# Sliding-window attention with a gated MLP: postponing the low parts of weights while VectorE has a result bank to empty, and a scratch buffer for each head's maxima

## The chip, the cores and the metric

The kernel runs on one core of a Trainium2 chip. A core has a matrix engine (TensorE, PE in the profile; its weight loads are shown as PEld), VectorE (DVE), ScalarE (ACT), GpSimd (POOL) and SyncE (SP), which here issues nearly all DMAs. Each engine works through its own queue in order; engines wait for each other, and for DMAs, through semaphores. The metric is the device time of one execution in microseconds, lower is better.

## The reference

```python
def _A_ref(x, wqkv, wo):                      # S = 2048, D = 640, H = 32, Dh = 20, W = 256
    qkv = (x @ wqkv).reshape(B, S, 3, H, Dh).transpose(2, 0, 3, 1, 4)
    scores = einsum("bhqd,bhkd->bhqk", q, k) * (Dh ** -0.5)
    mask = (idx[:, None] - idx[None, :] >= 0) & (idx[:, None] - idx[None, :] < W)
    p = softmax(where(mask, scores, -1e9))
    o = einsum("bhqk,bhkd->bhqd", p, v)
    return o.transpose(0, 2, 1, 3).reshape(B, S, D) @ wo

def _B_ref(x, w1, b1, w2, b2):                # F = 1536
    h = relu(x @ w1 + b1) ** 2
    return h @ w2 + b2

xn = layernorm(x)
return x + _A_ref(xn, wqkv, wo) * silu(_B_ref(xn, w1, b1, w2, b2))
```

All data are float32.

## The kernel before

Products are made from split numbers: every operand has a high part, rounded by ScalarE (a copy into fp32r), and a **low part**, the rest, made by VectorE or GpSimd (`raw - high`). A product takes three matmuls: high by high, high by low, low by high.

A first stage (to about 113 us) normalizes and transposes x, makes v and the first q and k. Then comes one long stage in which two kinds of work are interleaved on TensorE. The attention goes through 16 pairs of heads with 16 query tiles each, one tile a step of about 2 us: `scores` (L650) makes the scores of both heads of the pair in two banks `sps`; `maxima` (L658) on VectorE adds the mask and takes the row maximum, into the tile `mt`; its elementwise output `junk` is read by nobody. In the profile each maximum is two VectorE instructions: the pass itself and a read of the accumulator. Thirteen steps later `scores_t` makes transposed scores (`stps`, L690), `exps` on ScalarE (L696) and masks on GpSimd (L697, L699) make the probabilities, and every eight or so steps `values` (L731) does a burst of matmuls into the bank `ops`. A score bank is used again in the next step, so TensorE waits there for the maximum of the step before.

Between these, `filler` does the dense products in pieces: q and k of the later heads (`qkps`), the first layer of the MLP (`hps`) and the second (`yps`), all at L640 as halves of 64 rows, in three banks that take turns. A `Job` holds the second halves of a group; when its last one has been given out, `done` puts the bank's evacuation 0.25 (`SOON`) later. For `yps` the evacuation is `ysb = yps + bias` (or plus the first half's result, `yin`), on VectorE (L1185); for `qkps` it is `shm` on ScalarE (L1077) and `slo` on VectorE (L1080); for `hps` ScalarE (L1150). A group can start only when its bank has been emptied. After the loop a last stage makes the output product with wo (`wops`, from about 759 us).

The order on all engines is written out when the program is built, by a clock in the kernel's own code that adds up estimated costs (`clock`). `later(wait, fn)` puts a function down for a time of that clock, and `soon()` runs what is due. Weights arrive as pieces: `start_pieces` issues the load into one of three `raw` buffers (SyncE, L976), `go` makes the high part on ScalarE (L988, L997), and `subtract` puts the low parts (L991, L998) down for 1.9, 2.6, 3.3 ... after that, in `lows`. A raw buffer is free when all low parts of its piece have been made. `state[2]` is the step, 10**6 after the loop.

Of the kernel before, what the change touches and what calls it, by code (L numbers as in the profile page):

```python
# [11 lines left out]
BF16 = mybir.dt.bfloat16  # L12
# [3 lines left out]
P = 128  # L16
# [40 lines left out]
SOON = 0.25  # L57
# [9 lines left out]
def attn_mlp_kernel(ctx: ExitStack, tc, x, wqkv, wo, w1, b1, w2, b2, out):  # L67
# [9 lines left out]
    def mm_bank(shape, name):  # L77
        turn[0] = (turn[0] + 1) % 3
        return pmm.tile(shape, F32, tag=f"mm{turn[0]}", name=name)
# [62 lines left out]
    with tc.tile_pool(name="ph1v", bufs=2) as p1v, tc.tile_pool(name="ph1", bufs=2) as p1, tc.tile_pool(name="ph1x", bufs=4) as p1b, tc.tile_pool(name="ph1w", bufs=1) as p1w, tc.tile_pool(name="ph1t", bufs=2, space=PSUM) as p1t:  # L142
# [286 lines left out]
        with tc.manual_schedule(engines={E_.PE, E_.Activation, E_.DVE, E_.Pool, E_.SP}):  # L429
# [90 lines left out]
            for w in "kq":  # L520
                ps = pat.tile([P, BT // 2], F32, tag="s", name="qkps")
# [7 lines left out]
            for b in range(NB):  # L529
# [27 lines left out]
                for w in "kq":  # L557
                    ps = mm_bank([P, BT], "qkps")
# [25 lines left out]
    at2 = ctx.enter_context(tc.tile_pool(name="at2", bufs=2))  # L584
# [10 lines left out]
    backlog = deque()  # L595
    class Job:

        def __init__(self, done):
            self.items, self.after, self.done = deque(), None, done

    def put(j, emit, cost):
        clock[2] = clock[j]
# [21 lines left out]
    def drain(queue, jobs=99):  # L624
        end = max(0, len(queue) - jobs)
        while len(queue) > end:
            assert queue[0].after is not None
            behind(queue)
# [24 lines left out]

    def maxima(p, q, ss, nk):
        for hh in range(2):
            junk = at2.tile([P, 3 * P], BF16, tag="junk", bufs=1, name="junk")
            m = MG * hh + q % MG
            nc.vector.tensor_tensor_reduce(out=junk[:, :nk], in0=ss[hh][:, :nk], in1=mask[:, 3 * P - nk:], scale=1.0, scalar=-3.0e38, op0=ALU.add, op1=ALU.max, accum_out=mts[q // MG % 2][:, m:m + 1])  # L658

# [86 lines left out]
    state = [0.0, 0.0, 0]  # L746
# [3 lines left out]
    def post(dst, src, wait=0.0, then=lambda: None):  # L750
        def go():
            posts.append((dst, src))
            then()
        if whole[0] or not wait:
            go()
        else:
            later(wait, go)

    def post_all():
        for dst, src in posts:  # L760
            nc.sync.dma_start(dst, src)
        posts.clear()
# [9 lines left out]
    def later(wait, fn):  # L772
        tasks.append((clock[0] + wait, len(tasks), fn))
# [14 lines left out]
    def next_task():  # L788
        clock[0] = max(clock[0], min(tasks)[0])
        soon()  # L790
# [14 lines left out]
    def room():  # L805
        while state[2] < 10 ** 6 and not (banks and banks[0][0] < clock[0] + PATIENCE):
            yield None
# [17 lines left out]
    def halves(job, ps, a, b_, first, last, o=0, n=None):  # L825
        n = n or ps.n
        cost, out = COST[n], ps.tile[:, o:o + n]

        def front():
            job.mark = half(0, out, a, b_, start=first, stop=False)  # L830

        def back():
            if first:
                wait_for(job.mark)
            half(1, out, a, b_, start=False, stop=last)
        ahead(front, cost)
        job.items.append((back, cost))
        if last:
            job.after = clock[0]

    def open_job(evac, *then):
        def done():
            later(SOON, lambda: (post_all(), evac()))
            for f in then:
                f()
        job = Job(done)
        backlog.append(job)
        return job

    def mm_halves(ps, mms, work, evac, *then):  # L850
        job = open_job(evac, *then)
        for j, (a, b_) in enumerate(mms):
            halves(job, ps, a, b_, j == 0, j == len(mms) - 1)
            yield work
# [9 lines left out]
    def lin1(tiles, off, n):  # L864
        t, o = divmod(off, KC * BT)
        return tiles[t][:, o:o + n]
# [80 lines left out]
            item[1]()  # L947

    lows = []

    def subtract(tag, jobs):
        left = [len(jobs)]

        def put_off(k, job):
            def go():
                if item in lows:
                    lows.remove(item)
                    job()
                    left[0] -= 1
                    if not left[0]:  # L960
                        held[0] -= 1
            item = (tag, go)
            lows.append(item)
            later(1.9 + 0.7 * k, go)
        for k, job in enumerate(jobs):
            put_off(k, job)

# [83 lines left out]
    def filler():  # L1051
# [6 lines left out]
        for g, b in order_qk:  # L1058
# [9 lines left out]
            for w in "qk":  # L1068
                hi, lo = (t() for t in ws[g][w])
                yield from room()  # L1070
                ps = Acc(BT, "qkps")
# [13 lines left out]
                then = []  # L1085
                if b == 0 and w == "q":
                    then = [lambda g=g: shut.discard(f"g{g + 1}")]
                elif w == "k":
                    then = [lambda t=t: shut.discard(t) for t in opens.get((g, b), ())]
# [7 lines left out]
        def load_yin(i):  # L1097
            if i < NT:
                t = order[i]
                assert (0, t) in stored_y  # L1100
                yins[t] = wgt.tile([P, D], F32, tag="wgkh", name="yin")
                nc.sync.dma_start(yins[t], y_d[0][:, t, :])
        xb, its = [xT[p][NB - 1] for p in range(2)], []

        def late():
            j = lates[0]
            lates[0] += 1
            if j >= 3:
                load(0)
            if j >= 5:  # L1110
                load(1)
            if j >= 7:
                load(2)

        for n, (hf, b) in enumerate(blocks):
# [22 lines left out]
            for m, u in enumerate(parts):  # L1138
                yield from room()
                ps = Acc(BT, "hps")  # L1140
# [19 lines left out]
                job = open_job(evac, *([used] if m == len(parts) - 1 else []))  # L1160
# [10 lines left out]
            for tt in range(4):  # L1171
                t = b * 4 + tt
                place = [None]
                jobs = []

                def start(nh, hf=hf, t=t, place=place, idx=4 * (n - NB) + tt, end=n == NB - 1 and tt == 3, n=n, tt=tt):
                    sl = slice(nh * HALF, (nh + 1) * HALF)
                    ps = Acc(HALF, "yps")

                    def evac():  # L1180
                        vload[0] += 0.5
                        if not nh:
                            place[0] = room_of("p32", "ysb") if n == last else wgt.tile([P, D], F32, tag="wgqh", name="ysb")
                        ysb = place[0]
                        nc.vector.tensor_add(ysb[:, sl], ps.tile, (yins[t] if hf else b2t)[:, sl])  # L1185
                        ps.free(1.2)
                        if nh:
                            if n == last:
                                ybt[t] = ysb
                            else:  # L1190
                                post(y_d[hf][:, t, :], ysb, 1.0, lambda: stored_y.add((hf, t)))
                            if hf:
                                del yins[t]
                                load_yin(idx + 2)
                            if end:
                                shut.discard("21")
                    return [ps, open_job(evac), 0]

                def product(jb, nh, fc):
                    ps, job, _ = jb  # L1200
                    u = fc if fc < WIDE else (tt // 2, fc // 2)
                    o = tt * P if fc < WIDE else fc % 2 * MT + tt % 2 * P
                    while u not in made:
                        if state[2] < 10 ** 6:
                            yield None
                        elif tasks:
                            next_task()
                        else:
                            drain(backlog, 1)
                    for hp, wp in ((0, 0), (0, 1), (1, 0)):  # L1210
                        jb[2] += 1
                        halves(job, ps, hs[u][hp][:, o:o + P], lin1(wt2, (wp * NFH + fc) * D + nh * HALF, HALF), jb[2] == 1, jb[2] == 3 * NFH)
                        yield 0.133
                for nh in range(2):
                    yield from room()
                    if n == last:
                        late()
                    job = start(nh)
                    for fc in (*range(WIDE, NFH), *range(WIDE)) if tt < 2 else range(NFH):
                        yield from product(job, nh, fc)  # L1220
# [40 lines left out]
    def room_of(tag, name):  # L1261
        if tag == "p32":
            return at2.tile([P, 2, 3 * P], F32, tag="p32", bufs=PBUF, name=name).rearrange("p a n -> p (a n)")[:, :D]
        return wgt.tile([P, D], F32, tag=tag, name=name)
# [135 lines left out]
    due = [0.0]  # L1400
# [15 lines left out]
    with tc.manual_schedule(engines={E_.PE, E_.Activation, E_.DVE, E_.Pool, E_.SP}):  # L1416
# [7 lines left out]
        for s in range(steps):  # L1424
# [29 lines left out]
            if a:  # L1454
                maxima(*a, *sc)
# [51 lines left out]
```

## Time and profile before

| | us |
|---|---|
| median of 3 runs | 837.44 (837.16 to 837.87) |
| profiled execution | 838.13 |
| its span, first to last instruction | 836.4 |
| TensorE's granted clock | 1.0 throughout |

The profile is of the one execution of 838.13 us; its moments are microseconds from the start of its span. Lines such as L658 are lines of the kernel before; names are the kernel's own. "out<-in" tells what an instruction writes and reads. In a row of the order of time stand the start, the duration, the engine, the line and the operation, and in brackets how long the engine had been idle before it and who ended that; rows of equal neighbours are merged and carry their count. "2 us <- DVE" is an inference from semaphore events: where an instruction waits for several, it is put down to the latest event.

### The profile page before, as it was taken

Reading aid. Unit: us, or ns where it says so; the run is one execution under the profiler, and the core shown is the slowest. Engines: PE = TensorE matmul, PEld = TensorE weight load, DVE = VectorE, ACT = ScalarE, POOL = GpSimd, SP = SyncE. Lnnn points to the kernel's source line nnn. Section 1 sums busy time; section 2 is a strip of 40 time slices with the busy share of each in tenths; the row PEclk is TensorE's granted clock in tenths of the full one; section 3 lists DMA queues with packets and bytes.
Section 4 is the critical chain, followed back from the end, with each engine's and each line's share of the span. In section 5 each row is a group of like instructions: output and inputs, shape, how many; then the busy total and the mean of one; then the engine's idle time right before and its main releaser. Section 6 shows DMA issues by size and latency. Waiting matters only on the chain.

```text
span 836.4 us, 25137 instructions
## 1 busy us (share of the span) xinstructions
PE 826.2 (99%) x10082; PEld 779.0 (93%) x10082; DVE 477.8 (57%) x1398; ACT 425.5 (51%) x760; POOL 364.2 (44%) x672
## 2 busy tenths in 40 slices
PE   8999999999999999999999999999999999999997
PEld 8999999989889999999999989999999999999997
DVE  7855457656578455455455476655455455246763
ACT  6254323545566744744754754844644744664321
POOL 5177900334344542533542543643543643552442
PEclk9999999999999999999999999999999999999999
DMA  6999577878697555546083536585266557346962
GB/s 236 299 390 348 182 215 269 238 260 282 232 324 262 142 173 156 127 157 174 21 268 130 121 108 181 134 244 176 59 222 172 130 177 224 92 131 199 373 251 80
DMA packets 88812, 166.40 MB, mean 199 GB/s; under 512 B 10232, under 2 KB 36472, under 8 KB 87672
## 3 DMA queue, kind: packets, MB, share of 16 engines
q1 hardware_dynamic: 88536, 164.63, 62.7%
q8 instruction: 79, 1.29, 0.7%
q14 instruction: 37, 0.30, 0.1%
q10 hardware_dynamic: 160, 0.16, 0.1%
HBM read 93.66 MB, written 70.52 MB: 196 GB/s over the span
## 4 chain that ended last, share of the span: by engine, by line
PE 94%; DVE 2%; DMA 2%; issue 1%; ACT 1%; SPq 0%; POOL 0%; DVEq 0%; POOLq 0%; ACTq 0%
PE hps L640 20%; PE yps L640 20%; PE qkps L640 13%; PE ops L731 10%; PE wops L800 8%; PE stps L690 5%; PE sps L650 4%; PE vps L239 4%; PE qkps L214 3%; PE vps L362 3%; PE tps L181 1%; DVE junk L658 1%; DMA k_d<-slo 1%; DMA qs<-q_d 1%; PE vps L417 0%
## 5 line engine op out<-in xcount | busy, mean ns | idle before, releaser
L658 DVE CUSTOM_DVE_ANT_0 junk<-sps,mask 128x384 bf16<-128x384 f32 (+2 forms) x512 | 272.4, 532 | 250.9 <-PE sps L650 91.3
L696 ACT ACTIVATE p<-stps 128x768 f32<-128x768 f32 (+2 forms) x256 | 197.5, 772 | 255.5 <-PE stps L690 236.6
L697 POOL TENSOR_SCALAR_AFFINE_SELECT p<-p 128x256 f32<-128x256 f32 x256 | 109.8, 429 | 336.4 <-ACT p L696 334.0
L640 PE MATMUL yps<-w,hh 64*128 64x320 f32 x1536 | 226.1, 309 | 2.2 <-DVE ysb L1185 2.0
L640 PE MATMUL hps<-xb,w 64*128 64x256 f32 (+1 forms) x2100 | 210.0, 304 | 0.0
L640 PEld LDWEIGHTS hps<-xb,w 64*128 64x128 f32 x2100 | 194.7, 186 | 3.5 <-issue 2.7
L640 PEld LDWEIGHTS yps<-w,hh 64*128 64x128 f32 x1536 | 187.9, 185 | 7.3 <-DVE ysb L1185 4.4
L640 PE MATMUL yps<-w,hl 64*128 64x320 f32 x768 | 179.3, 308 | 0.0
L650 PE MATMUL sps<-ks,qs 60*128 60x384 f32 (+2 forms) x512 | 125.4, 335 | 1.0 <-DVE mt L658 1.0
L690 PE MATMUL stps<-qs,ks 62*128 62x384 f32 (+2 forms) x512 | 122.0, 334 | 0.1
L640 PEld LDWEIGHTS yps<-w,hl 64*128 64x128 f32 x768 | 121.4, 185 | 0.4 <-issue 0.4
L640 PE MATMUL qkps<-xT,wgqh 64*128 64x512 f32 x320 | 99.4, 391 | 0.0
L640 PE MATMUL qkps<-xT,wgkh 64*128 64x512 f32 x320 | 98.2, 391 | 0.0
L699 POOL TENSOR_SCALAR_AFFINE_SELECT p<-p 128x256 f32<-128x256 f32 x224 | 95.5, 426 | 0.0
L731 PE MATMUL ops<-p,vp 128*21 128x128 f32 (+1 forms) x2128 | 86.6, 311 | 0.0
L731 PEld LDWEIGHTS ops<-p,vp 128*21 128x21 f32 x2128 | 63.6, 101 | 21.2 <-issue 6.3
L650 PEld LDWEIGHTS sps<-ks,qs 60*128 60x128 f32 x512 | 78.4, 185 | 4.3 <-DVE mt L658 2.2
L690 PEld LDWEIGHTS stps<-qs,ks 62*128 62x128 f32 x512 | 77.5, 187 | 0.7 <-ACT p L696 0.6
L1155 POOL TENSOR_TENSOR hl<-sq,hh 128x512 fp32r<-128x512 f32 x48 | 62.1, 1293 | 16.1 <-ACT sq L1154 15.5
L800 PE MATMUL wops<-wo,oT 128*128 128x320 f32 (+2 forms) x384 | 62.0, 310 | 0.0
L640 PE MATMUL qkps<-xT,wgkl 64*128 64x512 f32 x160 | 61.4, 393 | 0.0
L640 PE MATMUL qkps<-xT,wgql 64*128 64x512 f32 x160 | 61.4, 390 | 0.0
(163 smaller groups left out, 1234.2 us busy)
## 6 DMA issues: line engine op xcount, KB each, us to landing
ks<-k_d SPq DMA_DIRECT2D x64, 240.0 KB
qs<-q_d SPq DMA_DIRECT2D x64, 240.0 KB
xb<-xs SPq DMA_DIRECT2D x60, 256.0 KB
k_d<-shm SPq DMA_DIRECT2D x20, 512.0 KB
q_d<-shm SPq DMA_DIRECT2D x20, 512.0 KB
xs<-xT SPq DMA_DIRECT2D x8, 1280.0 KB
y<-ysb SPq DMA_DIRECT2D x28, 320.0 KB
o<-osb SPq DMA_DIRECT2D x64, 128.0 KB
```

The costliest lines, as they stand in the source:

```text
L214: nc.tensor.matmul(ps, wt[:, c, :], xT[part][b][:, c * BT + t0:c * BT + t0 + n], start=m == 1, stop=m == 3 * KC)
L239: nc.tensor.matmul(ps, xT[xp][b][:, c * BT + t * P: c * BT + (t + 1) * P], wv[wp][:, c, nh * HALF:(nh + 1) * HALF], start=first and m == 0 ...
L640: return nc.tensor.matmul(out, a[r], b_[r], skip_group_check=True, **kw)
L650: nc.tensor.matmul(ss[hh][:, :nk], qs[i][o, q * P:(q + 1) * P], ks[i][o, k0 * P:k0 * P + nk], start=True, stop=True)
L658: nc.vector.tensor_tensor_reduce(out=junk[:, :nk], in0=ss[hh][:, :nk], in1=mask[:, 3 * P - nk:], scale=1.0, scalar=-3.0e38, op0=ALU.add, o ...
L690: nc.tensor.matmul(tps[:, hh, :n], ks[i][o, kb * P:(kb + 1) * P], qs[i][o, kb * P:kb * P + n], start=True, stop=True)
L696: nc.scalar.activation(p32[:, :, :n], tps[:, :, :n], AF.Exp, scale=SCALE)
L697: nc.gpsimd.affine_select(p32[:, :, 0:P], p32[:, :, 0:P], pattern=[[0, 2], [1, P]], compare_op=ALU.is_ge, fill=0.0, base=0, channel_multip ...
L699: nc.gpsimd.affine_select(p32[:, :, 2 * P:], p32[:, :, 2 * P:], pattern=[[0, 2], [-1, P]], compare_op=ALU.is_gt, fill=0.0, base=0, channel ...
L731: nc.tensor.matmul(ot[r0:r0 + VW, c0:c0 + len(part), :], vps[p][:, kb // 4, kb % 4, hh, :], pts[p, kb][:, hh, :].rearrange("p (t n) -> p t ...
L800: nc.tensor.matmul(ps, a, b_, start=j == 0, stop=j == n - 1)
L1155: nc.gpsimd.tensor_sub(hh[1][:, :BT], sq, f32(hh[0]))
```

## The change

`maxima` gives each of the two heads a scratch buffer of its own, `junk0` and `junk1`, in place of one `junk`. Jobs of `yps` are marked `vector`. While such a job's evacuation is due but not yet given out (`vector_evacs`), or while the oldest waiting job is one of them with less than 0.7 of second halves left, `pressing()` is true, and a low part that comes due is put down again for 0.4 later. `ensure`, which forces low parts out ahead of their use, calls `go()` without `due` and isn't put off. After the loop nothing is put off.

```diff
-            junk = at2.tile([P, 3 * P], BF16, tag="junk", bufs=1, name="junk")
+            junk = at2.tile([P, 3 * P], BF16, tag=f"junk{hh}", bufs=1, name="junk")
...
-    def open_job(evac, *then):
+    def open_job(evac, *then, vector=False):
+        def finished():
+            post_all()
+            evac()
+            vector_evacs[0] -= vector
+
         def done():
-            later(SOON, lambda: (post_all(), evac()))
+            vector_evacs[0] += vector
+            later(SOON, finished)
             for f in then:
                 f()
         job = Job(done)
+        job.vector = vector
...
+    vector_evacs = [0]
+
+    def pressing():
+        job = backlog[0] if backlog else None
+        return state[2] < 10 ** 6 and (vector_evacs[0] or job and job.vector and job.after is not None and sum(c for _, c in job.items) < 0.7)
 
     def subtract(tag, jobs):
         left = [len(jobs)]
 
         def put_off(k, job):
-            def go():
+            def go(due=False):
                 if item in lows:
+                    if due and pressing():
+                        later(0.4, lambda: go(True))
+                        return
                     lows.remove(item)
...
-            later(1.9 + 0.7 * k, go)
+            later(1.9 + 0.7 * k, lambda: go(True))
...
-                    return [ps, open_job(evac), 0]
+                    return [ps, open_job(evac, vector=True), 0]
```

On TensorE, ScalarE, GpSimd and SyncE every instruction stands where it stood. Only VectorE's queue differs. Of its 512 maxima, 512 named VectorE's own semaphore (DVE_49) among what they wait for, and now 23 do; with that, 488 of VectorE's instructions that only wait are gone. And low parts change places with `ysb` in three spots. In the rows, `ISA` with `junk` is a maximum, `ISA` with `mt` alone its accumulator read; `w_1_1` are tiles of MLP weights; line numbers of the changed kernel are 15 higher from L991 on.

VectorE near 485 us of the profile, before:

```order
L658 ISA junk,mt_101<-sps,mask 128x384 [waits DVE_49,PE_49]
L658 ISA mt_101 128x1
L658 ISA junk,mt_101<-sps,mask 128x384 [waits DVE_49,PE_49]
L658 ISA mt_101 128x1
L991 TENSOR_TENSOR w_1_1_8514<-raw,w_1_0_8470 128x384 [waits DMAHW6_49,Activation_49]
L991 TENSOR_TENSOR w_1_1_8514<-raw,w_1_0_8470 128x384
L1185 TENSOR_TENSOR ysb<-yps,b2t 128x320 [waits DMAHW5_49,PE_49]
```

and now:

```order
L658 ISA junk,mt_101<-sps,mask 128x384 [waits PE_49]
L658 ISA mt_101 128x1
L658 ISA junk,mt_101<-sps,mask 128x384 [waits PE_49]
L658 ISA mt_101 128x1
L1200 TENSOR_TENSOR ysb<-yps,b2t 128x320 [waits DMAHW5_49,PE_49]
L1006 TENSOR_TENSOR w_1_1_8530<-raw,w_1_0_8470 128x384 [waits DMAHW6_49,Activation_49]
L1006 TENSOR_TENSOR w_1_1_8530<-raw,w_1_0_8470 128x384
```

The two maxima no longer wait for VectorE itself, and the `ysb` went ahead of two low parts. Near 497 us a `ysb` went ahead of one low part in the same way. The third spot is VectorE near 735 us, before:

```order
L998 TENSOR_TENSOR wo_13552<-raw,wo_13551 128x640
L1185 TENSOR_TENSOR ysb<-yps,yin 128x320
L998 TENSOR_TENSOR wo_13552<-raw,wo_13551 128x640 x2
L1185 TENSOR_TENSOR ysb<-yps,yin 128x320
L1256 RECIPROCAL rec<-rec 128x128
```

and now:

```order
L1200 TENSOR_TENSOR ysb<-yps,yin 128x320
L1013 TENSOR_TENSOR wo_13552<-raw,wo_13551 128x640 x2
L1200 TENSOR_TENSOR ysb<-yps,yin 128x320
L1271 RECIPROCAL rec<-rec 128x128
L1013 TENSOR_TENSOR wo_13552<-raw,wo_13551 128x640
```

Three low parts of wo each went behind the `ysb` next to them, the third behind a reciprocal too. TensorE near 320 us, the same in both kernels:

```order
L640 MATMUL yps<-w_0_2_3948,hh 128x320
L650 MATMUL sps<-ks_1473,qs_1472 128x384 [waits DMAHW1_49,DMAHW0_49,DVE_49]
L650 MATMUL sps<-ks_1473,qs_1472 128x384 [waits DMAHW3_49,DMAHW2_49,DVE_49]
L690 MATMUL stps<-qs_116,ks_117 128x384 [waits Activation_49]
L690 MATMUL stps<-qs_116,ks_117 128x384
L665 MATMUL stps<-ident,mt_100 64x64 x2
```

Here the scores of a new half of a pair begin; their matmuls wait for the loads of q and k (DMAHW) beside VectorE. Nothing moved there.

More of the change, by code (lines that the diff above doesn't have):

```diff
@@ L598, in __init__ @@
         def __init__(self, done):
-            self.items, self.after, self.done = deque(), None, done
+            self.items, self.after, self.done, self.vector = deque(), None, done, False
     def put(j, emit, cost):
```

## The prediction

> **What bounds the kernel now.** I read the page first, for the busiest engine and the chain that ended last; then the list of waits; then the order of time around each wait of TensorE.
>
> ```profile
> span 836.4 us, 25137 instructions
> PE 826.2 (99%) x10082; PEld 779.0 (93%) x10082; DVE 477.8 (57%) x1398; ACT 425.5 (51%) x760; POOL 364.2 (44%) x672
> PE 94%; DVE 2%; DMA 2%; issue 1%; ACT 1%; SPq 0%; POOL 0%; DVEq 0%; POOLq 0%; ACTq 0%
> ```
>
> TensorE is busy for 826.2 of 836.4 us and the chain lies on it for 94%. Its work is the same after the change, and so is its order. VectorE works 57% of the span, so making it faster is worth nothing by itself: the change can give back only idle time of TensorE that VectorE ends. The list of waits names that time (total, times, longest):
>
> ```profile
> PEld yps L640 <- DVE ysb L1185: 4.4, 9, 1.3
> PEld sps L650 <- DVE mt L658: 2.2, 5, 1.0
> ```
>
> I count the idle time of PEld, the weight load, since a matmul that waits begins by loading its weights. The ceiling is thus 4.4 + 2.2 = 6.6 us, 0.8% of the time. Here are the 14 waits one by one, from the order of time; in the brackets stands how long the load waited, and for whom:
>
> ```profile
> 159.71 0.18 PEld L650 LDWEIGHTS sps<-ks,qs 60*128 60x128 f32 x1 [0.28 <-DVE mt L658]
> 245.63 0.18 PEld L650 LDWEIGHTS sps<-ks,qs 60*128 60x128 f32 x1 [0.53 <-DVE mt L658]
> 320.02 0.18 PEld L650 LDWEIGHTS sps<-ks,qs 60*128 60x128 f32 x1 [0.96 <-DVE mt L658]
> 364.49 0.29 PEld L640 LDWEIGHTS yps<-w,hh 64*128 64x128 f32 x3 [0.30 <-DVE ysb L1185]
> 377.67 0.18 PEld L640 LDWEIGHTS yps<-w,hh 64*128 64x128 f32 x1 [0.40 <-DVE ysb L1185]
> 428.88 0.19 PEld L640 LDWEIGHTS yps<-w,hh 64*128 64x128 f32 x2 [0.18 <-DVE ysb L1185]
> 438.92 0.18 PEld L640 LDWEIGHTS yps<-w,hh 64*128 64x128 f32 x1 [0.26 <-DVE ysb L1185]
> 488.00 0.18 PEld L640 LDWEIGHTS yps<-w,hh 64*128 64x128 f32 x1 [1.26 <-DVE ysb L1185]
> 495.33 0.18 PEld L640 LDWEIGHTS yps<-w,hh 64*128 64x128 f32 x1 [0.72 <-DVE ysb L1185]
> 505.24 0.18 PEld L640 LDWEIGHTS yps<-w,hh 64*128 64x128 f32 x1 [0.59 <-DVE ysb L1185]
> 560.39 0.29 PEld L640 LDWEIGHTS yps<-w,hh 64*128 64x128 f32 x3 [0.44 <-DVE ysb L1185]
> 617.97 0.19 PEld L640 LDWEIGHTS yps<-w,hh 64*128 64x128 f32 x2 [0.21 <-DVE ysb L1185]
> 647.38 0.18 PEld L650 LDWEIGHTS sps<-ks,qs 60*128 60x128 f32 x1 [0.20 <-DVE mt L658]
> 699.37 0.18 PEld L650 LDWEIGHTS sps<-ks,qs 60*128 60x128 f32 x1 [0.22 <-DVE mt L658]
> ```
>
> **Part one: a scratch buffer for each head.** With one buffer, the second maximum of a pair waits on VectorE's own semaphore until the first has written. What that costs is to be seen in a pair whose scores lie ready, followed by a ysb:
>
> ```profile
> 314.08 0.56 DVE L658 CUSTOM_DVE_ANT_0 junk<-sps,mask 128x384 bf16<-128x384 f32 x1 [0.99 <-PE sps L650]
> 314.56 0.08 DVE L658 DVE_READ_ACCUMULATOR2_ANT mt<- 128x1 f32 x1
> 314.79 0.56 DVE L658 CUSTOM_DVE_ANT_0 junk<-sps,mask 128x384 bf16<-128x384 f32 x1
> 315.27 0.08 DVE L658 DVE_READ_ACCUMULATOR2_ANT mt<- 128x1 f32 x1
> 315.27 0.48 DVE L1185 TENSOR_TENSOR ysb<-yps,b2t 128x320 f32<-128x320 f32 x1
> ```
>
> From the first maximum to the second it is 314.79 - 314.08 = 0.71 us; from the second to the ysb, which does not wait for it, 315.27 - 314.79 = 0.48. No row shows a maximum behind a maximum without the wait. The bounds of the saving are therefore 0 (something else holds the second one) and 0.71 - 0.48 = 0.23; if it starts when the accumulator has been read (314.56 + 0.08), it is 0.15. I take 0.23, because the nearest row, the ysb, follows the same instructions without the wait and starts with the accumulator's read.
>
> The Trainium skill speaks against this part: "VectorE: DVE Perf Modes", section "The DRAIN you can't avoid", says that the next op starts only when the pipe is empty, and that eight copies took the same time with a semaphore behind each as with one behind the last. By that rule the 0.23 is 0, part one gives nothing, and the sum below shrinks to part two alone. The ysb row above disagrees with it: 0.48 against 0.71.
>
> Over 256 pairs it is up to 59 us of VectorE, nearly all hidden: VectorE just waits longer for the next scores. On the path it counts where a TensorE wait ends behind a pair that TensorE's scores had started. First and last of seven such ysb (364, 377, 428, 438, 495, 560, 617):
>
> ```profile
> 363.95 0.48 DVE L1185 TENSOR_TENSOR ysb<-yps,b2t 128x320 f32<-128x320 f32 x1
> 617.43 0.49 DVE L1185 TENSOR_TENSOR ysb<-yps,yin 128x320 f32<-128x320 f32 x1
> ```
>
> Each ends about 0.05 before the load that waited, and each gets 0.23, no more than its wait: 0.23 + 0.23 + 0.18 + 0.23 + 0.23 + 0.23 + 0.21 = 1.54. The wait at 495.33 keeps 0.49, since four low parts stay ahead of its ysb:
>
> ```profile
> 492.90 1.98 DVE L991 TENSOR_TENSOR w<-raw,w 128x128 fp32r<-128x128 f32 x4
> ```
>
> At 505.24 two pairs run ahead of the ysb, with two low parts between them and no gap, so 2 x 0.23 = 0.46 of 0.59:
>
> ```profile
> 502.23 1.37 DVE L991 TENSOR_TENSOR w<-raw,w 128x384 fp32r<-128x384 f32 x2
> ```
>
> Of the waits for a score bank, 159.71 gives 0.23 (one pair, behind a slo that ScalarE released) and 699.37 gives 0.22, all it has. At 245.63 two pairs lie ahead:
>
> ```profile
> 242.57 1.23 DVE L991 TENSOR_TENSOR w<-raw,w 128x384 fp32r<-128x384 f32 x2
> 243.72 0.68 DVE L1080 TENSOR_TENSOR slo<-qkps,shm 128x512 fp32r<-128x512 f32 x1
> 242.73 0.60 ACT L1077 ACTIVATE shm<-qkps 128x512 fp32r<-128x512 f32 x1
> ```
>
> The slo needs the shm, which ends at 243.33; 0.23 earlier it would start at 243.49, so it moves along, and the wait loses 0.46 of 0.53. Two waits get nothing. At 647.38 the maximum that is waited for had itself waited for TensorE:
>
> ```profile
> 646.76 0.56 DVE L658 CUSTOM_DVE_ANT_0 junk<-sps,mask 128x384 bf16<-128x384 f32 x1 [0.49 <-PE hps L640]
> 319.07 0.08 DVE L658 DVE_READ_ACCUMULATOR2_ANT mt<- 128x1 f32 x1
> ```
>
> At 320.02 the bank had been free since 319.07 + 0.08 = 319.15; that instruction (in the order above: it names two DMA semaphores beside VectorE's) waited 0.87 us longer for the next pair's q and k. I count 0 of its 0.96. Part one: 1.54 + 0.46 + 0.23 + 0.22 + 0.46 = 2.91 us, or at 0.15 a pair 1.95.
>
> **Part two: low parts put off.** Three places move. At 488.00:
>
> ```profile
> 485.47 2.08 DVE L991 TENSOR_TENSOR w<-raw,w 128x384 fp32r<-128x384 f32 x2
> 487.47 0.48 DVE L1185 TENSOR_TENSOR ysb<-yps,b2t 128x320 f32<-128x320 f32 x1
> 486.70 0.30 PE L640 MATMUL yps<-w,hh 64*128 64x320 f32 x1
> ```
>
> The ysb now stands ahead of the two low parts. If its sums are ready it starts at 485.24 and the load, due at 488.00 - 1.26 = 486.74, no longer waits: 1.26. The row only proves that TensorE's last product ended by 487.00; a ysb that had to wait for that would save 0.47. Ends 0.47 and 1.26; I take 1.26, since the load was held for this very ysb and the emission of a ysb follows its last product. The two low parts end about half a us later than 487.55 at most, with the burst of ops behind them, where no scores come. At the second place (near 497) a ysb passes a low part; no wait of TensorE is listed there, so 0. At the third, in the last 100 us, ysb pass low parts of wo; the listed waits hold no VectorE wait of a weight load there, so 0 too. DMAs: a low part frees a raw slot for the next weight's load on SyncE's queue, so that load can be up to half a us later; nothing on TensorE's list waits for one.
>
> **The sum.** 2.91 + 1.26 = 4.17 us off the profiled execution's 838.13 (its span of 836.4 and 1.7 around it): 833.96. That execution lay 0.69 above the median of the runs, 837.44, so the forecast is 837.44 - 4.17 = 833.3 us, 0.50% less. At 0.15 a pair it is 837.44 - 1.95 - 1.26 = 834.2. If every VectorE wait vanished, 4.4 + 2.2 - 0.96 = 5.6 less, 831.8.
>
> **Rivals.**
> - *The second maximum is held anyway* (pair saving 0). For it: no row shows the pair without its wait. Against it: 0.48 against 0.71 above. Only part two is left: 836.2, within 0.2%; with the 0.47, 837.0. If the low parts' move yields nothing either, no change. Chance 0.15 for both.
> - *TensorE arrives earlier only to wait for another.* For it: the q and k wait at 320.02 is there already, and ScalarE's exponentials end waits too:
>
> ```profile
> 537.29 0.19 PEld L690 LDWEIGHTS stps<-qs,ks 62*128 62x128 f32 x2 [0.41 <-ACT p L696]
> SPq L886 <- PE stps L690: 19.2, 17, 3.6
> SPq L976 <- DVE w L991: 41.0, 9, 11.0
> ```
>
> Against it: the queue that loads q and k waits for TensorE in 17 places, so the loads come earlier with it, and ScalarE at 51% follows TensorE as well. If the 0.69 gained ahead of 320.02 is lost there and half of the rest, about (4.17 - 0.69) / 2 = 1.7 remains: 835.7. Chance 0.20.
> - *Slower: a low part put off holds the queue of loads.* SyncE stood 41.0 us behind low parts in nine places, once 11.0, with stores and q and k loads queued behind. If the move lengthens such a stand so that the next pair's q and k are late by more than the 4.17 gained, the kernel loses; with half of an 11 us stand in the open (5.5) it would be 837.44 - 4.17 + 5.5 = 838.8, and it exceeds 0.2% from 5.9 us on. Against it: the moved low parts end at most half a us later. Chance 0.04.
>
> **How the numbers follow.** About 0.2%, 1.7 us, is what a measurement of this kernel can tell from no change; faster therefore means below 835.8. The forecast, with a saving of 0.15 to 0.23 a pair and up to the ceiling (831.8 to 834.3), has 0.61; the second rival 0.20, three quarters of it below 835.8; the first 0.15, all within; the slower one 0.04. Faster 0.61 + 0.15 = 0.76, same 0.05 + 0.15 = 0.20, slower 0.04. The range goes from the ceiling, 831.8, to the first rival's 836.2, rounded up to 836.4.
>
> **What would show it.** In the profile after, the second maximum starts 0.48 us behind the first (0.56 if the read holds it, 0.71 if the rule holds). The wait of 1.26 is gone, the list reads about 1.1 us for yps on ysb instead of 4.4, and about 1.3 for sps on mt, of which 0.96 is the q and k wait. TensorE's busy time stays at 826. The prediction is wrong if those waits shrink and the span doesn't, with new waits for ACT, DMA or POOL in the list, or if the pitch stays at 0.71.

## The result, and the profile after

The changed kernel takes 831.4 us (median of six runs, 830.63 to 831.5) against 837.46 for the kernel before, run beside it: 6.06 us less, a ratio of 0.9923 with a 95% interval of 0.9911 to 0.9936. The forecast was 4.17 us less, 833.3; the time lies 0.4 below the low end of the range. The profiled execution took 831.43 us.

The page's lines on the span, the engines and the chain of the changed kernel:

```profile
span 829.7 us, 24649 instructions
PE 822.3 (99%) x10082; PEld 777.8 (94%) x10082; DVE 456.8 (55%) x1398; ACT 425.2 (51%) x760; POOL 361.6 (44%) x672
PE 97%; DVE 1%; ACT 1%; DMA 0%; issue 0%; ACTq 0%
```

VectorE is busy 21.0 us less, and the chain lies on TensorE for 97% instead of 94%. The line that surprises is the first of the engines: the span fell by 6.7 us, and TensorE's *busy* time by 3.9 of these, from 826.2, with the same 10,082 matmuls in the same order.

Of the list of waits after, the rows for the same weight loads (total, times, longest):

```profile
PEld yps L640 <- DVE ysb L1200: 0.7, 2, 0.5
PEld sps L650 <- DVE mt L658: 0.5, 2, 0.2
PEld sps L650 <- issue: 0.3, 1, 0.3
```

The first two were 4.4 and 2.2 before. The third is the load that waited 0.96 us at 320.02; it stood under `mt` then and is listed without a releaser now. So 6.6 - 1.5 = 5.1 us of listed waits are gone, of a span that is 6.7 shorter.

The order of time around 684 us of the changed kernel: a pair, its ysb, and two rows of loads.

```profile
683.92 0.56 DVE L658 CUSTOM_DVE_ANT_0 junk<-sps,mask 128x384 bf16<-128x384 f32 x1 [1.46 <-PE sps L650]
684.40 0.55 DVE L658 CUSTOM_DVE_ANT_0 junk<-sps,mask 128x384 bf16<-128x384 f32 x1
684.88 0.48 DVE L1200 TENSOR_TENSOR ysb<-yps,yin 128x320 f32<-128x320 f32 x1
685.22 0.30 PEld L640 LDWEIGHTS yps<-w,hl 64*128 64x128 f32 x2
685.42 0.40 PEld L640 LDWEIGHTS yps<-w,hh 64*128 64x128 f32 x4
```

The second maximum starts 0.48 us behind the first, while the accumulator of the first is being read. Over all 224 pairs of full width with nothing between their maxima, that distance was 0.71 us in the middle before and is 0.48 now, and none is over 0.484. The same place in the kernel before:

```profile
690.41 0.56 DVE L658 CUSTOM_DVE_ANT_0 junk<-sps,mask 128x384 bf16<-128x384 f32 x1 [1.22 <-PE sps L650]
691.12 0.56 DVE L658 CUSTOM_DVE_ANT_0 junk<-sps,mask 128x384 bf16<-128x384 f32 x1
691.61 0.48 DVE L1185 TENSOR_TENSOR ysb<-yps,yin 128x320 f32<-128x320 f32 x1
691.72 0.31 PEld L640 LDWEIGHTS yps<-w,hl 64*128 64x128 f32 x2
692.14 0.30 PEld L640 LDWEIGHTS yps<-w,hh 64*128 64x128 f32 x4
```

This is the place to learn from. The `hl` loads end at 692.03, the ysb at 692.09, and the next load starts at 692.14: TensorE waited 0.11 us for VectorE, and the row has no bracket, because the profile shows none for an idle time this short. After the change the `hh` load starts at 685.42, 0.10 *before* the `hl` loads end (685.52): loads for the two halves of TensorE's rows overlap. So the place gained about 0.2 us (0.17 by the loads around it): more than the idle time that the rows before show, and nothing of it stands in the list of waits.

At 488 us the ysb stands ahead of the two low parts, and no load waits for it any more:

```profile
482.37 0.48 DVE L1200 TENSOR_TENSOR ysb<-yps,b2t 128x320 f32<-128x320 f32 x1
482.77 1.91 DVE L1006 TENSOR_TENSOR w<-raw,w 128x384 fp32r<-128x384 f32 x2
```

In what follows "load by load" means that the 10,082 weight loads of two profiles, which stand in the same order but for neighbours that start within a few hundredths of a microsecond of each other, are laid side by side, and the difference of their starts is followed: where it jumps, time was gained or lost.

### The profile page after: what moved, and what is told of

The parts are those of the page before. It is cut to its first block, busy times and chain, and to the rows that moved or that the text cites. A ratio compares the mean times of both kernels' runs of the same rounds, so it can differ in the third digit from the quotient of the medians.

```text
span 829.7 us, 24649 instructions
## 1 busy us (share of the span) xinstructions
PE 822.3 (99%) x10082; PEld 777.8 (94%) x10082; DVE 456.8 (55%) x1398; ACT 425.2 (51%) x760; POOL 361.6 (44%) x672
## 3 DMA queue, kind: packets, MB, share of 16 engines
q8 instruction: 79, 1.29, 0.7%
## 4 chain that ended last, share of the span: by engine, by line
PE 97%; DVE 1%; ACT 1%; DMA 0%; issue 0%; ACTq 0%
PE yps L640 21%; PE hps L640 20%; PE qkps L640 14%; PE ops L731 10%; PE wops L800 9%; PE stps L690 5%; PE sps L650 5%; PE vps L239 4%; PE qkps L214 3%; PE vps L362 3%; PE tps L181 1%; PE vps L417 0%; PE vps L407 0%; DMA xt<-in_A_x_dram 0%; DVE st L157 0%; DVE w L1006 0%
## 5 line engine op out<-in xcount | busy, mean ns | idle before, releaser
L658 DVE CUSTOM_DVE_ANT_0 junk<-sps,mask 128x384 bf16<-128x384 f32 (+2 forms) x512 | 252.1, 530 | 256.6 <-PE sps L650 108.2
L697 POOL TENSOR_SCALAR_AFFINE_SELECT p<-p 128x256 f32<-128x256 f32 x256 | 107.8, 421 | 331.6 <-ACT p L696 329.1
L640 PE MATMUL yps<-w,hh 64*128 64x320 f32 x1536 | 225.1, 309 | 0.3 <-DVE ysb L1200 0.2
L640 PE MATMUL hps<-xb,w 64*128 64x256 f32 (+1 forms) x2100 | 210.9, 304 | 0.0
L640 PEld LDWEIGHTS hps<-xb,w 64*128 64x128 f32 x2100 | 196.8, 186 | 3.3 <-issue 2.7
L640 PEld LDWEIGHTS yps<-w,hh 64*128 64x128 f32 x1536 | 185.9, 185 | 3.6 <-issue 2.3
L640 PE MATMUL yps<-w,hl 64*128 64x320 f32 x768 | 175.7, 308 | 0.0
L650 PE MATMUL sps<-ks,qs 60*128 60x384 f32 (+2 forms) x512 | 129.6, 333 | 0.1
L690 PE MATMUL stps<-qs,ks 62*128 62x384 f32 (+2 forms) x512 | 127.3, 331 | 0.2 <-ACT p L696 0.2
L640 PEld LDWEIGHTS yps<-w,hl 64*128 64x128 f32 x768 | 117.8, 185 | 0.4 <-issue 0.4
L640 PE MATMUL qkps<-xT,wgqh 64*128 64x512 f32 x320 | 99.4, 391 | 0.0
L640 PE MATMUL qkps<-xT,wgkh 64*128 64x512 f32 x320 | 98.1, 391 | 0.0
L699 POOL TENSOR_SCALAR_AFFINE_SELECT p<-p 128x256 f32<-128x256 f32 x224 | 94.9, 424 | 0.0
L690 PEld LDWEIGHTS stps<-qs,ks 62*128 62x128 f32 x512 | 82.1, 187 | 1.2 <-ACT p L696 0.6
L650 PEld LDWEIGHTS sps<-ks,qs 60*128 60x128 f32 x512 | 81.2, 185 | 2.1 <-DVE mt L658 0.5
L640 PE MATMUL qkps<-xT,wgql 64*128 64x512 f32 x160 | 61.3, 390 | 0.0
L640 PE MATMUL qkps<-xT,wgkl 64*128 64x512 f32 x160 | 61.2, 392 | 0.0
```

What stands on the lines that cost most here:

```text
L640: return nc.tensor.matmul(out, a[r], b_[r], skip_group_check=True, **kw)
L650: nc.tensor.matmul(ss[hh][:, :nk], qs[i][o, q * P:(q + 1) * P], ks[i][o, k0 * P:k0 * P + nk], start=True, stop=True)
L690: nc.tensor.matmul(tps[:, hh, :n], ks[i][o, kb * P:(kb + 1) * P], qs[i][o, kb * P:kb * P + n], start=True, stop=True)
L697: nc.gpsimd.affine_select(p32[:, :, 0:P], p32[:, :, 0:P], pattern=[[0, 2], [1, P]], compare_op=ALU.is_ge, fill=0.0, base=0, channel_multip ...
L699: nc.gpsimd.affine_select(p32[:, :, 2 * P:], p32[:, :, 2 * P:], pattern=[[0, 2], [-1, P]], compare_op=ALU.is_gt, fill=0.0, base=0, channel ...
```

## Experiments

The theory after the result: both mechanisms are as forecast, and what was missed are many waits for VectorE too short for the list. The rivals: the excess came from the new order of the low parts, or from loads that landed earlier.

**The two buffers alone.** The kernel before with this line of the change:

```diff
-            junk = at2.tile([P, 3 * P], BF16, tag="junk", bufs=1, name="junk")
+            junk = at2.tile([P, 3 * P], BF16, tag=f"junk{hh}", bufs=1, name="junk")
```

> The kernel before with the two scratch buffers alone; the low parts keep their places, so 23 second maxima are still followed at once by low parts and the 1.26 us wait at 488 stays or shrinks by one pair's 0.23. Theory (the pair's 0.23 us reaches TensorE at every wait for VectorE, also at those under about 0.15 us which the list of waits leaves out, and the two parts add up): gain about 5.0 us, 832.4 against 837.5. The prediction's own sum for this part alone: 2.9 us, 834.5. If the second maximum were held by VectorE's pipe whatever the buffer: 837.5. If the gain beyond the sum came from the new order of the low parts: no more than 2.9 us.

832.3 us against 837.34 (ratio 0.9942, 0.9929 to 0.9956): 5.0 us. The 1.26 us at 488 stay whole, and almost all else is gone from the list:

```profile
PEld yps L640 <- DVE ysb L1185: 1.9, 3, 1.3
484.82 0.18 PEld L640 LDWEIGHTS yps<-w,hh 64*128 64x128 f32 x1 [1.26 <-DVE ysb L1185]
```

The excess over the forecast is in this part, with no low part moved. That rules out their order as its source.

**The low parts put off, alone.** The changed kernel with the line above undone.

> The changed kernel with one scratch buffer for both heads again: the low parts are put off, and each second maximum waits for the first to end, pitch 0.71 us. Theory: the 1.26 us wait at 488 goes and nothing else does, 836.2 us. If the gain beyond the sum (about 2 us) came from the order of the low parts or from loads that are issued earlier: about 834.2. If both parts must be there for the wait at 488 to go: 837.4.

836.09 us against 837.34 (ratio 0.9982, 0.9974 to 0.9991): 1.25 us, where the sum had 1.26. Load by load the place at 488 gave 1.29. The parts add up: 5.04 + 1.25 = 6.3 against 6.06 together.

**The wait given back in the counted pairs, and in all others.** The changed kernel, with one buffer for both heads in some pairs only. The first run does it in the 13 pairs that stand ahead of the waits counted in the sum, the second (`not in`) in the other 243. No instruction changes its place.

```diff
+    mxcount, COUNTED = [0], {20, 55, 56, 106, 111, 133, 137, 159, 163, 164, 187, 211, 245}
...
+        mxcount[0] += 1
+        one = mxcount[0] - 1 in COUNTED
...
-            junk = at2.tile([P, 3 * P], BF16, tag=f"junk{hh}", bufs=1, name="junk")
+            junk = at2.tile([P, 3 * P], BF16, tag=f"junk{0 if one else hh}", bufs=1, name="junk")
```

> The changed kernel with one scratch buffer for both heads again, but only in the 13 pairs of maxima (of 256) that stand ahead of the waits which the prediction's sum counted; the order of all instructions is that of the changed kernel. The prediction's sum: these 13 pairs hold all that the buffers bring, 2.91 us given back, 831.4 + 2.9 = 834.3. Theory of many small waits: 2.7 us given back (what the changed kernel and the one with the put-off alone differ by at these places, load by load), 834.1. If the gain were a matter of order or of loads: 831.4.

> The opposite half: one scratch buffer in the other 243 pairs, two in the 13 that were counted. The prediction's sum: nothing given back, since no wait for VectorE that the list shows stands behind these pairs, 831.4. Theory of many small waits: about 2.0 us given back (4.7 for all pairs less 2.7 for the 13), 833.4.

834.39 us for the 13 (ratio 0.9964, 0.9951 to 0.9976) and 833.47 for the 243 (0.9955, 0.9943 to 0.9968; the changed kernel's interval ends at 0.9936). Against 831.4 the 13 pairs cost 3.0 us, where the sum had 2.91, and the 243 cost 2.1, where it had nothing. The second run's list of waits, and its page:

```profile
PEld sps L650 <- DVE mt L662: 1.7, 6, 0.4
PEld yps L640 <- DVE ysb L1204: 0.9, 3, 0.5
PE 824.7 (99%) x10082; PEld 779.4 (94%) x10082; DVE 477.4 (57%) x1398; ACT 425.2 (51%) x760; POOL 362.8 (44%) x672
```

VectorE's busy time is nearly that of the kernel before (477.8). TensorE's has risen by 2.4 us over the changed kernel, and by 0.5 only (to 822.8) in the run with the 13 pairs, which lost more: most of what the 243 pairs cost is booked as work and not as idle time, where a held load loses its overlap with its neighbour. (The profile models when a matmul ends, so its busy time is no exact measure.) Load by load between the run with the low parts put off alone, which has one buffer throughout, and the changed kernel, over 20 places outside the counted ones gain 0.04 to 0.32 us each, about 2 us together. About 0.3 of that is the place of 647.38, whose listed wait the sum had set to 0; nearly all the others have no wait in the list. That the uncounted pairs cost 2 us with the order unchanged is the cause of the miss, and this is shown.

Which place costs how much isn't the same in every run. In the second run's profile the place of 647.38 lost nothing, while 0.38 was lost at 472 and 0.19 at 201, behind two pairs that took 1.06 us there and about 0.7 in the three profiles with one buffer throughout (last section). They are two of the six waits in its list.

**Is the wait at 320 the kernel's?** The sum gave nothing to the 0.96 us at 320.02, as a wait for a load of q and k. In the changed kernel's first profile the same wait was 0.31. So the kernel before was profiled again, unchanged.

> The kernel before, profiled once more. The prediction counted 0 for the 0.96 us wait at 320.02; the profiles of the changed kernel and of four others show 0.31, 0, 0.55, 0 and 0.10 there. If the wait is set by when a load of keys and queries lands and that scatters between executions, it will be another here, 0 to 0.6 us. If the change shortened it, it is 0.9 to 1.0 us again.

837.13 us, span 835.4 (836.4 in the first). The loads of the two score banks around the place, in the second profile of the kernel before, then in the first of the changed kernel and, last, in its second:

```profile
318.79 0.18 PEld L650 LDWEIGHTS sps<-ks,qs 60*128 60x128 f32 x1
319.25 0.18 PEld L650 LDWEIGHTS sps<-ks,qs 60*128 60x128 f32 x1
```

```profile
317.72 0.18 PEld L650 LDWEIGHTS sps<-ks,qs 60*128 60x128 f32 x1
318.35 0.18 PEld L650 LDWEIGHTS sps<-ks,qs 60*128 60x128 f32 x1 [0.31 <-issue]
```

```profile
317.64 0.18 PEld L650 LDWEIGHTS sps<-ks,qs 60*128 60x128 f32 x1
317.92 0.18 PEld L650 LDWEIGHTS sps<-ks,qs 60*128 60x128 f32 x1
```

The second load has no bracket in the repeated kernel before: it waited 0.14 us, for VectorE, and the 0.82 us that the place lost in the first profile are the only jump over 0.15 between the two. In the changed kernel it waited 0.31 in one execution and not at all in another. The landing of the load is a matter of the execution, up to 0.8 us, and belongs to no change. Apart from it, the pair gives the place another 0.14 to 0.18.

**More yielding.** The changed kernel with low parts put off earlier (a serial number breaks ties in the list of due functions):

```diff
-        return state[2] < 10 ** 6 and (vector_evacs[0] or job and job.vector and job.after is not None and sum(c for _, c in job.items) < 0.7)
+        return state[2] < 10 ** 6 and (vector_evacs[0] or job and job.vector and job.after is not None and sum(c for _, c in job.items) < 2.0)
```

> The changed kernel with the threshold by which a low part is put off raised from 0.7 to 2.0 units of the planner, so that low parts stand behind more of the bias additions. Theory: the largest wait that is left, 0.49 us at 490.93 for a bias addition, goes, and perhaps the 0.17 at 375.46: 0.4 to 0.6 us under the changed kernel, about 831.0. Rival: the low parts come late for their own matmuls or hold raw loads on SyncE's queue, and the time is the same or 0.5 us longer.

833.72 us (0.9958, 0.9945 to 0.997): 2.3 slower than the changed kernel, worse than the rival said, which was 0.5. The rows of the score bank behind the ysb, then of the last stage:

```profile
491.78 0.40 PEld L650 LDWEIGHTS sps<-ks,qs 60*128 60x128 f32 x2 [0.67 <-DVE mt L658]
...
740.79 0.81 DVE L1014 TENSOR_TENSOR wo<-raw,wo 128x640 fp32r<-128x640 f32 x1
741.46 0.60 SPq L988 DMA_DIRECT2D raw<-in_A_wo_dram  x1
745.03 0.74 ACT L1013 ACTIVATE wo4h<-raw 128x640 fp32r<-128x640 f32 x1 [3.66 <-DMA raw<-in_A_wo_dram]
746.31 0.18 PEld L690 LDWEIGHTS stps<-qs,ks 62*128 62x128 f32 x2 [1.65 <-ACT p L696]
```

The low part at 740.79 is late, so its raw buffer comes free late, the load is issued at 741.46 (733.17 at the latest in the changed kernel), and ScalarE stands 3.66 us before the copy, with the exponentials queued behind it that empty TensorE's next bank. That is the mechanism of the prediction's slow rival, a low part that holds the loads; the change itself stays short of it. At 490 the ysb gained 0.63, but five low parts behind it held the next pair of maxima, and 0.98 was lost at the banks.

**Yielding a little more.** The same with a threshold of 1.1, once, and once more beside the changed kernel.

> The changed kernel with the threshold at 1.1 units, not 0.7 and not 2.0: the bias addition at 490.93 goes ahead of four low parts and another ahead of one, and the last stage keeps the order of the changed kernel. In the run with 2.0 the last stage lost 1.7 us to a copy that waited for its raw load, and the wait at 490.93 came back as 0.67 us at the next score bank. If that is so, this kernel loses nothing at the end and gains nothing at 490.93: 831.2 to 831.7. If the bank's wait was due to what 2.0 moved earlier at that place, the 0.49 us is gained: 830.9.

> The changed kernel once more, as the control beside the one with the threshold at 1.1, on the same chip: 831.4 us as before. The wait for the load of keys and queries near 318 was 0.31 us in its first profile; it will be another, 0 to 0.6.

> The kernel with the threshold at 1.1 beside the changed kernel on the same chip. Load by load its first profile was 0.33 us shorter around 490 (0.63 gone at the bias addition, 0.30 back at the next score bank), 0.12 at 692, and 0.34 at the load of keys and queries, which the threshold does not touch. Theory: only the first two are the kernel's, 0.3 to 0.45 us under the changed kernel. Rival: the whole 0.8 us by which the two medians differ. Rival: no difference, two chips.

830.62 us the first time (0.9919, 0.9906 to 0.9933). Side by side, 830.57 (0.9919, 0.9906 to 0.9933) and 831.57 for the changed kernel (0.9929, 0.9915 to 0.9942). Medians 0.8 and 1.0 apart, intervals that overlap: that it is faster is likely, not settled. Load by load both profiles agree on 0.33 us at 490 (0.63 gained at the ysb, 0.30 given back at the bank), and that is all that can be laid to the order. The rest went to and fro with the load of q and k, whose wait was 0.42 in the repeated run.

**A third instruction between the maxima.** The changed kernel, with one line in 240 pairs, once with this subtraction and once with `nc.vector.memset(ones, 1.0)` in its place; nothing reads the result.

```diff
+            if not hh and p:
+                nc.vector.tensor_sub(ones, ident[0:2, :], ident[0:2, :])
```

> The changed kernel with one small subtraction of VectorE (its result is read by nothing) between the two maxima of 240 of the pairs; a subtraction of 128x128 took 0.20 us in the trace, so each of these pairs is about as long as with the self-wait, and no other order or buffer changes. Theory (only VectorE's time for a pair counts): the gain of the two buffers is given back nearly whole, 835.5 to 836.2 us. Rival (only the listed waits count, as the prediction's sum had it): 2.5 to 2.9 us given back, 834.0. Rival (the gain comes from order or loads): stays within 0.5 us of the changed kernel.

> The run with the small subtraction came out at 837.7 us, 1.6 above the one with the put-off alone, although a pair of maxima with it is usually 0.68 us long, not 0.71. Its trace shows subtractions of up to 1.3 us that end with a tensor operation of GpSimd, where most take 0.28. This kernel has a memset of the same 2x128 in the same 240 places, which reads nothing. Theory: the excess came from waiting for GpSimd's operation, so no memset is long beside GpSimd, GpSimd's own busy time stays at about 362 us, and 2.5 to 4.5 us are given back: 834.0 to 836.0. Rival: any third instruction between the two maxima costs the same, 837.7.

The subtraction cost more than the self-wait had: 837.73 us (1.0006, 0.9997 to 1.0014), outside all three expectations. The memset cost nothing: 831.42 (0.9932, 0.9918 to 0.9945), also outside. Rows of the first:

```profile
281.54 1.30 POOL L1172 TENSOR_TENSOR hl<-sq,hh 128x512 fp32r<-128x512 f32 x1
281.77 1.21 DVE L660 TENSOR_TENSOR ones<-ident 2x128 f32<-2x128 f32 x1
282.91 0.54 DVE L658 CUSTOM_DVE_ANT_0 junk<-sps,mask 128x384 bf16<-128x384 f32 x1
```

and of the second:

```profile
313.14 0.56 DVE L658 CUSTOM_DVE_ANT_0 junk<-sps,mask 128x384 bf16<-128x384 f32 x1 [1.15 <-PE sps L650]
313.67 0.17 DVE L660 MEMSET ones<- 2x128 f32 x1
313.76 0.48 DVE L658 CUSTOM_DVE_ANT_0 junk<-sps,mask 128x384 bf16<-128x384 f32 x1
314.18 0.47 DVE L1202 TENSOR_TENSOR ysb<-yps,b2t 128x320 f32<-128x320 f32 x1
```

The subtraction usually took 0.28 us and put the maxima 0.69 apart, near the old 0.71; but here it ran from 281.77 to 282.98, and GpSimd's operation ended at 282.84. In 29 of 224 full pairs the maxima were over 0.73 apart, up to 1.71. All 33 subtractions that took over 0.30 us ended 0.14 to 0.15 us behind the end of an operation of GpSimd. The memset never was long (0.17), and no pair was over 0.624. It even lengthens a pair with its ysb only from 0.96 us (684.88 - 683.92) to 1.04 (314.18 - 313.14), since the maximum behind it takes 0.42 to the next start, not 0.48. The expectation for the memset went by the distance between the maxima, not by what the whole pair grows. Load by load the memset lost 0.05 to 0.07 at some ten places and gained 0.35 at 490, for a reason of its own (last section). So waiting for GpSimd is most of the difference between the two and not all of it: of the 6.3 us, 4 to 5 were lost where a subtraction was long. The rest goes with the length of the pair: from its first maximum to the instruction behind the second it is usually 1.16 us with the subtraction, 1.04 with the memset and 1.19 with one buffer. That VectorE's time for a pair counts is shown by the buffers given back; these two runs agree with it, but mix it with GpSimd.

## Why the prediction was right or wrong

- *The pair's 0.23 us*: right, 0.71 to 0.48, and not 0.56. The rival in which the second maximum is held anyway, and with it the rule of the Trainium skill weighed there, fails. The Trainium skill, "VectorE: DVE Perf Modes", section "Two Vector instructions with no wait between them", says that a held instruction starts only when every earlier one has finished, which leaves one that isn't held free to start sooner; the trace agrees, with a start 0.08 us before the first maximum ends (684.40 against 683.92 + 0.56).
- *The counted pairs, 2.91 us*: right; giving them back cost 3.0. Single terms missed: load by load 505.24 gained 0.58, not 0.46, and 159.71 gained 0.15, not 0.23. At 699.37 a wait of 0.23 was still there in the first profile, although that place lost 0.30 when the 13 pairs were given back. The pair there follows a ysb that itself waits for an earlier ysb's store to land, in the kernel before and in the changed one:

```profile
697.64 0.49 DVE L1185 TENSOR_TENSOR ysb<-yps,yin 128x320 f32<-128x320 f32 x1 [1.32 <-DMA y<-ysb]
691.16 0.49 DVE L1200 TENSOR_TENSOR ysb<-yps,yin 128x320 f32<-128x320 f32 x1 [1.80 <-DMA y<-ysb]
```

In the changed kernel's second profile VectorE stood 1.73 us before that ysb and the load behind the pair waited 0.16; with the two buffers alone VectorE stood 1.34 and the load didn't wait. So 0.22 for every execution was taken from one here too, and the good total of 2.91 hides terms that missed both ways.
- *Low parts, 1.26 us*: right, 1.25 alone.
- *The ceiling*: this is the step that failed. "The change can give back only idle time of TensorE that VectorE ends" and "The list of waits names that time" both fall short. The list leaves out waits of up to about 0.15 us, and a load that is held loses its overlap with the neighbouring load before any idle time appears. The 243 pairs that the sum left at 0 measured 2.1 us (the wait at 647.38 among them); 4.17 + 2.1 = 6.3 against the 6.06 seen. The ceiling of 5.6, and the low end of the range that was set by it, fell with that. "TensorE's busy time stays at 826" was the same error once more: it went to 822.3.
- *0 for 647.38*: wrong, it gained 0.30. The bracket `[0.49 <-PE hps L640]` was read as a wait for TensorE. The pair there took 1.06 us from maximum to maximum in both profiles of the kernel before, and TensorE's signal, as recorded, had come 0.41 before the second one started. Two buffers make it 0.49:

```profile
639.79 0.56 DVE L658 CUSTOM_DVE_ANT_0 junk<-sps,mask 128x384 bf16<-128x384 f32 x1 [2.83 <-PE hps L640]
640.28 0.55 DVE L658 CUSTOM_DVE_ANT_0 junk<-sps,mask 128x384 bf16<-128x384 f32 x1
```

- *0 for 320.02*: the reading as a wait for loads was right. That its 0.96 us stood for every execution was taken from one, and wasn't so.
- *TensorE arrives earlier only to wait for another*: the longest wait for ScalarE stayed at about 0.4, no new wait came, and the gain stands to the end.

## What to carry to other kernels

Where one engine runs at 99%, the list of waits isn't the ceiling of what a faster neighbour can give back. Take off what another cause holds as well (here the 0.96 us at 320.02), and add the places where that neighbour's last instruction ends within a few hundredths of a microsecond before a load that waits for it, with or without a bracket. To find out, give the cost back in part of the places only, with the order unchanged, and lay the two traces side by side. Profile the unchanged kernel twice before a wait is priced that a DMA ends, or that stands behind an instruction which a DMA holds.

## What the runs showed of the hardware

In these traces VectorE and GpSimd stand in each other's way where both read SBUF. Four low parts of the changed kernel (the first row), with GpSimd's masks beside them:

```profile
488.51 1.97 DVE L1006 TENSOR_TENSOR w<-raw,w 128x128 fp32r<-128x128 f32 x4
488.80 0.59 POOL L697 TENSOR_SCALAR_AFFINE_SELECT p<-p 128x256 f32<-128x256 f32 x1 [3.14 <-ACT p L696]
489.35 0.72 POOL L699 TENSOR_SCALAR_AFFINE_SELECT p<-p 128x256 f32<-128x256 f32 x1
```

and the same four in the run with the memset, which began 0.09 later:

```profile
488.60 1.55 DVE L1008 TENSOR_TENSOR w<-raw,w 128x128 fp32r<-128x128 f32 x4
488.81 1.60 POOL L699 TENSOR_SCALAR_AFFINE_SELECT p<-p 128x256 f32<-128x256 f32 x1 [3.13 <-ACT p L698]
```

In one they take turns, with masks of 0.59 and 0.72 us where 0.41 is usual; in the other the mask is held for 1.60 us and the low parts go through in 1.55. That is the 0.35 us by which this run gained at 490. The Trainium skill, "SBUF — State Buffer", section "Who interferes with whom", says that a VectorE instruction with two inputs in SBUF contends with a GpSimd instruction that reads SBUF, and calls the port pair that they share an exclusive lock. The subtraction of 1.21 us beside GpSimd agrees; the memset, which reads nothing, was never long.

Three pairs of the kernel before, at 421.57, 646.76 and 693.98, took 1.06 us in three profiles with one buffer throughout (their moments are a little earlier in the other two) and 0.48 with two. In the run with 243 pairs on one buffer these three took about 0.7, and two others, at 200.32 and 471.53, took 1.06. What held them beyond their own wait stays open.
